# Background loads earlier and begun by ScalarE, high parts a step ahead of low parts

## The chip, the cores and the metric

The kernel runs on one core of a Trainium2 chip. The metric is the device time of one execution in microseconds (us). Five engines work beside each other, each through its own list of instructions in order: TensorE (PE in the profile; its weight loads are PEld), VectorE (DVE), ScalarE (ACT), GpSimd (POOL) and SyncE (SP), which only begins transfers. A transfer can be begun by SP or by ACT; each has a queue of its own, and the same 16 DMA engines move the bytes of both.

## The reference, cut to what matters

One transformer block for 2048 tokens of width 576, in float32. A vector `c` gives six modulation rows, attention has 32 heads of 128 that look at the last 512 cached keys (two heads share a cache), and a gated MLP of width 4608 follows.

```python
mod = (_silu(c) @ w_mod).reshape(c.shape[0], 6, 1, -1)
sa, ca, ga, sb, cb, gb = (mod[:, k] for k in range(6))
h = _layernorm(x) * (1 + ca) + sa
q = (h @ wq) per head
p = softmax(q @ k_cache[last 512] * Dh ** -0.5)
x = x + ga * ((p @ v_cache[last 512]) @ wo)
h = _layernorm(x) * (1 + cb) + sb
x = x + gb * ((sigmoid(h @ w_gate) * (h @ w_up)) @ w_down)
```

## The kernel before, in words

Each float32 product is made of three products of float32r parts: a value is split into a high part (ScalarE copies it rounded) and a low part (VectorE or GpSimd subtracts the high part from the value). The large products also use a seven-product scheme over 2 x 2 blocks (Strassen's), so weights are first added and subtracted with each other (the sums s1 to s4, t1 to t4) and then split.

The program is one loop over steps `n`, written out at build time. Steps -224 to -1 are the query projection (`q_step`, 7 products of 7 matmuls for each of 32 weight units). Steps 0 to 511 are attention, four steps for each block of 512 queries of one head: three matmuls of scores (`st`), four transposes of the probabilities (`pt`), three matmuls with the values (`ot`). After step 511 come the output projection and the MLP. Until then every engine keeps the order in which the program was written: `at_n(n, fn, ...)` puts a function at a step, ahead of that step's own products, and `at_late` behind them.

In one attention step ScalarE makes the exponentials (`pp<-st,neg`) and the rounded copy of the transposed probabilities (`ptt<-pt`), VectorE the maximum (`neg<-st`) and the low part of `ptt`, GpSimd the low part of the next queries (`qt`). Once in four steps the reciprocal sums `rs` go to a scratch in memory (`rscr<-rs`, `put_rs`) and come back spread over the partitions (`rb<-rscr`, `get_rs`); VectorE then multiplies the result `ot` by `rb` into `ov` (`ov_out`), and `put_o` stores `ov`.

Beside this runs background work, which prepares weights of later stages: 36 chunks `ab` of the gate and up weights, 9 chunks `tail` with their last rows, 16 `wo` and 18 `down` (these two are called wide here). A chunk has a room (a 128 x 2304 buffer: the `x` tiles and, in attention, four more called `xr`) or two. `bg_load` begins 4 transfers, `bg_sums` makes the sums on GpSimd in two parts, `bg_split` splits on ScalarE and GpSimd in two parts (not for `ab`), and `bg_store` begins 1 transfer (`ab`), 2 (wide) or 24 in four steps (`tail`, 6 in each step) to the scratches `wsc`, `wosc` and `dsc`. A planner sets the steps: a chunk is started at `n` when rooms are free and its due time is past, rooms are held for `HOLD` steps, and the due time moves on by a number for each kind. In the kernel before, all 636 of these transfers are begun by SP, between its other ones.

Weight units of the query projection are loaded raw by `load_raw` and `load_first` (SP), added by `w_sums` (GpSimd) and split by `w_split` (ScalarE, and right behind it VectorE). Finished queries go out by `q_store` (SP), from four buffers `qo`. `mod_fetch` loads one modulation row's weights (`wm`), `mod_sum` scales and adds them (ScalarE, GpSimd), and `mod_make2` ends with a matmul `st<-wm,ones`.

Of the kernel before, what the change touches and what calls it, by code (L numbers as in the profile page):

```python
# [16 lines left out]
P = 128  # L17
# [27 lines left out]
def adaln_block_kernel(ctx: ExitStack, tc: tile.TileContext, x, k_cache, v_cache, wq, wo, w_gate, w_up, w_down,  # L45
                       c, w_mod, out):
    early = [True]
    nc = Ordered(tc, early, tc.nc)
# [12 lines left out]
    D2 = D // 2  # L61
# [32 lines left out]
    def f32(ap):  # L94
        return ap.bitcast(F32)

    TQ = D2 - 2 * P
# [9 lines left out]
    def pin(i):  # L107
        if not early[0]:
            tc.keep_in_program_order(i)
# [4 lines left out]
    RAW = [qw.tile([P, 3, 4, P], F32, tag=f"raw{i}", name=f"raw{i}") for i in range(2)]  # L114
# [121 lines left out]
    A11, A12, A22, S1, S2, S4, S3, A21 = range(8)  # L236
# [55 lines left out]
    EARLY = 14  # L292
# [19 lines left out]
    WS, SWQ = {}, {}  # L312
# [11 lines left out]
            eng.tensor_sub(t[:, :, 0], raw_of(u, A12), WS[u, 0][:, :, 1])  # L324
            eng.tensor_sub(t[:, :, 1], raw_of(u, A11), raw_of(u, A21))

    def w_split(u, names, src, tail=None):
        tail = tail or nc.vector
        n = len(names)
        t = sw_tile([P, 5, 2, P]) if n == 2 else qw.tile([P, 5, 1, P], F32R, tag="sa", name="sa", bufs=2)  # L330
        nc.scalar.activation(t[:, 0:3], src, AF.Copy)
        nc.vector.tensor_sub(t[:, 3:5], src[:, 0:2], f32(t[:, 0:2]))
        r = slice(2 * TQ, 3 * TQ)
        tail.tensor_sub(t[r, 2], src[r, 2], f32(t[r, 2]))
        for i, a in enumerate(names):
            SWQ[u, a] = t[:, :, i, :]

    def w_split_first(u):
        w_split(u, (A11, A12), RAW[u // 2 % 2][:, :, u % 2 :: 2, :], nc.gpsimd if u else None)

    def w_split_a(u):
        w_split(u, (A11, A12), RAW[(u + 1) % 2][:, :, 0::2, :])

    def w_split_s(u, k):
        w_split(u, ((S1, S2), (S4, S3))[k], WS.pop((u, k)))

    def w_split_last(u):
        w_split(u, (A22,), RAW[(u + 1) % 2][:, :, 3:4, :])
# [151 lines left out]
    cols = {(h, s): ps_st() if 3 * h + s < 4 else ps_c() if s == 1 else ps_a() for h in range(2) for s in range(3)}  # L500
# [13 lines left out]
    for k in range(6):  # L514
        src = shift[0:1, k // 3 * D2 + k % 3 * P : k // 3 * D2 + (k % 3 + 1) * P] if k % 3 < 2 else \
# [13 lines left out]
    def at_n(n, fn, *args):  # L529
        at_step.setdefault(n, []).append((fn, args))  # L530
# [4 lines left out]
    def q_n(i):  # L535
        return NLO + i
# [15 lines left out]
    assert len(order) == NQ  # L552
    place = {x_: q_n(i) for i, x_ in enumerate(order)}
    for u in range(2, EARLY):
        at_n(max(place[u, A11] - 3, q_n(0)), w_split_first, u)
        if u >= 4:
            at_n(place[u // 2 * 2, A11] - 7, load_first, u)
    for u in range(2 * HKV):
        if u < EARLY:
            n = place[u, S1]  # L560
            at_n(n - 8, load_raw, u)
            times = (n - 4, n - 3), (n - 2, n), n + 1
        else:
            n = place[u, A11]
            at_n(n - (8 if u == EARLY else 10), load_raw, u)
            at_n(n - 3, w_split_a, u)
            times = (n - 4, n - 2), (n - 1, n + 1), n + 3
        for k in range(2):
            at_n(times[0][k], w_sums, u, k)
            at_n(times[1][k], w_split_s, u, k)  # L570
        at_n(times[2], w_split_last, u)


    CH = {}
# [441 lines left out]
    def bg_load(k, rooms):  # L1016
        kind, f = k
        if kind == "tail":
            raw = bg_view(rooms[0], 0, [4, P])
            BG[k] = raw, bg_view(rooms[0], 4 * P, [4, P]), bg_view(rooms[0], 8 * P, [7, P])  # L1020
            for slot, w, r0 in ((0, w_gate, 2 * P), (1, w_gate, D2 + 2 * P), (3, w_up, 2 * P), (2, w_up, D2 + 2 * P)):
                src = w[r0 : r0 + TQ, f * P : (f + 4) * P].rearrange("r (q n) -> q r n", q=4)
                pin(nc.sync.dma_start(raw[:, slot, :], src))
        elif kind == "ab":
            r = BG[k] = bg_view(rooms[0], 0, [8, 2, P])
            cols = slice(f * P, (f + 1) * P)
            for slot, w, r0 in ((0, w_gate, 0), (1, w_gate, D2), (2, w_up, D2), (7, w_up, 0)):
                pin(nc.sync.dma_start(r[:, slot], w[r0 : r0 + 2 * P, cols].rearrange("(s p) n -> p s n", p=P)))
        else:
            r = bg_view(rooms[0], 0, [8, D2])  # L1030
            BG[k] = r, bg_view(rooms[1], 0, [8, D2])
            w = wo if kind == "wo" else w_down
            for half, to in enumerate(((0, 1), (5, 2) if kind == "wo" else (7, 2))):
                for c, slot in enumerate(to):
                    r0 = (2 * f + c) * P
                    pin(nc.sync.dma_start(r[:, slot], w[r0 : r0 + P, half * D2 : (half + 1) * D2]))

    def bg_sums(k, part):
        kind, f = k
# [45 lines left out]
    def bg_store(k, part):  # L1085
        kind, f = k
        if kind == "tail":
            hi = BG[k][2]
            q = part
            rows = slice(q * TQ, (q + 1) * TQ)  # L1090
            for to in range(4):
                for a, b, src in bg_pairs(k) if to % 2 else [(0, 7, hi)]:
                    pin(nc.sync.dma_start(wsc[f + q][to * TQ : (to + 1) * TQ, a:b, 2, :], src[rows]))
        elif part == 0:
            if kind == "ab":
                pin(nc.sync.dma_start(wsc[f][:, :, 0:2], BG[k][:, 0:7]))
                return
            n = 8 if k == ("down", NF // 2 - 1) else 7
            for i in range(2):
                to = wosc[f // 4][:, :, f % 4, i].rearrange("c p d -> p c d") if kind == "wo" else dsc[f][:, i, :n]  # L1100
                pin(nc.sync.dma_start(to, BG[k][1 - i][:, :n]))


    XR = 4
# [5 lines left out]
    SPANS = {r: [(NLO + 27, NLO + 83), (ROOMS_FREE, N - 42)] if r < 2 else [(ROOMS_FREE, N - 42)] for r in range(NB)}  # L1110
    for r in range(NB, NB + XR):
        SPANS[r] = [(2, N - 42)]
    HOLD = {"ab": 14, "tail": 22, "wo": 22, "down": 22}
    free = {r: SPANS[r][0][0] for r in SPANS}
    n = NLO + 27
    due = float(n)
    while jobs or wide:
        assert n < N - 44, (n, len(jobs), len(wide))

        def fits(kind):  # L1120
            return [r for _, r in sorted((free[r], r) for r in SPANS if free[r] <= n and
                                         any(lo <= n and n + HOLD[kind] <= hi for lo, hi in SPANS[r]))]
# [24 lines left out]
    for b in range(NB):  # L1147
        at_n(max(free[b], N - 48 + 4 * b), load_x, b)
# [698 lines left out]
```

## Time and profile before

| what | value |
|---|---|
| median of 3 runs | 3193.76 us (3190.1 to 3196.66) |
| the profiled execution | 3193.45 us, its span 3191.5 us |
| granted TensorE clock, mean | 0.981 |
| PE busy | 3014.5 us (94%) |
| DVE, ACT, POOL busy | 2251.4 (71%), 1818.9 (57%), 1854.6 us (58%) |
| bytes moved | 637.28 MB, 200 GB/s over the span |
| first and last maximum of the scores | at 486.7 and 1571.8 us |

Nearly every instruction is recorded at line 36, a helper, so groups are told apart by their tiles. A name like `ptt<-pt` is output and input. The bracket behind a row of the timeline is the idle time ahead of it and what ended it. A DMA instruction's duration is the time that its queue (SPq, ACTq) spent on beginning it, not the transfer.

### The profile page before, as it was taken

Reading aid. Unit: us, or ns where it says so; the run is one execution under the profiler, and the core shown is the slowest. Engines: PE = TensorE matmul, PEld = TensorE weight load, DVE = VectorE, ACT = ScalarE, POOL = GpSimd, SP = SyncE. Lnnn points to the kernel's source line nnn. Section 1 sums busy time; section 2 is a strip of 40 time slices with the busy share of each in tenths; the row PEclk is TensorE's granted clock in tenths of the full one; section 3 lists DMA queues with packets and bytes.
Section 4 is the critical chain, followed back from the end, with each engine's and each line's share of the span. In section 5 each row is a group of like instructions: output and inputs, shape, how many; then the busy total and the mean of one; then the engine's idle time right before and its main releaser. Section 6 shows DMA issues by size and latency. Waiting matters only on the chain.

```text
span 3191.5 us, 50573 instructions
## 1 busy us (share of the span) xinstructions
PE 3014.5 (94%) x16375; PEld 2567.4 (80%) x16375; DVE 2251.4 (71%) x3908; ACT 1818.9 (57%) x3663; POOL 1854.6 (58%) x1685
## 2 busy tenths in 40 slices
PE   8878988789989998989999999999999999999999
PEld 6666766677777776777799998888888888888888
DVE  6767556667877776778788777666666686666667
ACT  5455446778878786767644555444444544444443
POOL 3745554578888885432255503676665566655555
PEclk9999999999999999999999999999999999999999
DMA  5855887878888888887654775655655565555554
GB/s 172 246 178 178 249 233 208 242 223 251 254 276 271 256 277 230 230 231 203 224 196 157 296 244 171 176 160 165 171 140 146 163 189 150 144 139 147 141 138 120
DMA packets 510087, 637.28 MB, mean 200 GB/s; under 512 B 56192, under 2 KB 429824, under 8 KB 501120
## 3 DMA queue, kind: packets, MB, share of 16 engines
q1 hardware_dynamic: 508688, 633.53, 66.5%
q8 instruction: 131, 2.15, 0.3%
q14 instruction: 132, 1.08, 0.1%
q10 hardware_dynamic: 1136, 0.53, 0.1%
HBM read 426.64 MB, written 207.25 MB: 199 GB/s over the span
## 4 chain that ended last, share of the span: by engine, by line
PE 63%; DMA 12%; DVE 7%; ACT 5%; issue 4%; POOL 4%; SPq 3%; ACTq 0%; POOLq 0%; DVEq 0%
PE a L36 22%; PE w L36 12%; PE c L36 11%; PE b L36 6%; PE ot L36 5%; PE st L36 4%; SPq L36 3%; DMA rb<-rscr 3%; PE pt L36 3%; DMA rscr<-rs 2%; DVE sw L36 2%; ACT pp L36 1%; ACT ptt L36 1%; DMA raw<-in_A_wq_dram 1%; POOL x L36 1%
## 5 line engine op out<-in xcount | busy, mean ns | idle before, releaser
L36 DVE TENSOR_TENSOR x<-w,x 128x288 f32<-128x288 f32 x964 | 418.8, 451 | 239.3 <-PE w L36 235.7
L36 PE MATMUL a<-hc,sw 128*128 128x512 f32 x2016 | 585.1, 396 | 1.4 <-DVE v L36 1.3
L36 PE MATMUL ot<-ptt,vs 128*128 128x512 f32 x1536 | 451.4, 403 | 56.2 <-DVE ptt L36 56.0
L36 PE MATMUL st<-kt,qt 128*128 128x512 f32 x1536 | 493.3, 430 | 3.0 <-POOL qt L36 3.0
L36 DVE TENSOR_TENSOR ptt<-pt,ptt 128x512 fp32r<-128x512 f32 x512 | 352.6, 689 | 191.6 <-ACT ptt L36 190.0
L36 ACT ACTIVATE pp<-st,neg 128x512 f32<-128x512 f32 x512 | 352.0, 687 | 175.2 <-DVE neg L36 172.3
L36 PEld LDWEIGHTS ot<-ptt,vs 128*128 128x128 f32 x1536 | 289.4, 192 | 143.6 <-DVE ptt L36 78.7
L36 PEld LDWEIGHTS a<-hc,sw 128*128 128x128 f32 x2016 | 356.4, 188 | 42.1 <-DVE v L36 3.2
L36 ACT ACTIVATE sw<-sr 128x384 fp32r<-128x384 f32 x504 | 257.4, 518 | 192.0 <-issue 90.5
L36 DVE TENSOR_REDUCE neg<-st 128x1 f32<-128x512 f32 x512 | 348.5, 681 | 6.2 <-PE st L36 6.2
L36 POOL TENSOR_TENSOR sw<-sr,sw 128x256 fp32r<-128x256 f32 x245 | 184.6, 754 | 281.0 <-ACT sw L36 276.0
L36 ACT ACTIVATE ptt<-pt 128x512 fp32r<-128x512 f32 x512 | 303.8, 593 | 77.0 <-PE pt L36 74.5
L36 PEld LDWEIGHTS pt<-ident,pp 128*128 128x128 f32 x2048 | 259.9, 143 | 100.1 <-ACT pp L36 29.8
L36 PEld LDWEIGHTS w<-wh,hl 128*128 128x128 f32 x1776 | 297.1, 188 | 52.7 <-DVE x L36 3.1
L36 PE MATMUL pt<-ident,pp 128*128 128x128 f32 x2048 | 313.5, 276 | 26.8 <-DVE rs L36 17.9
L36 PE MATMUL w<-wh,hl 128*128 128x288 f32 x1776 | 328.2, 296 | 0.8 <-DVE x L36 0.7
L36 POOL TENSOR_TENSOR qt<-qr,qt 128x512 fp32r<-128x512 f32 x128 | 165.8, 1295 | 273.4 <-ACT qt L36 191.3
L36 PE MATMUL c<-hc,sw 128*128 128x512 f32 x1008 | 304.0, 395 | 0.0
L36 DVE TENSOR_TENSOR sw<-sr,sw 128x256 fp32r<-128x256 f32 x259 | 187.9, 726 | 141.9 <-ACT sw L36 138.6
L36 PEld LDWEIGHTS st<-kt,qt 128*128 128x128 f32 x1536 | 256.4, 193 | 29.0 <-POOL qt L36 3.6
L36 POOL TENSOR_TENSOR hl<-vs,hl 128x512 fp32r<-128x512 f32 x139 | 191.8, 1380 | 108.1 <-ACT hl L36 106.1
L36 POOL TENSOR_TENSOR x<-x 128x256 f32<-128x256 f32 (+3 forms) x226 | 178.1, 805 | 74.4 <-DMA x<-in_B_w_up_dram 45.9
(295 smaller groups left out, 5895.9 us busy)
## 6 DMA issues: line engine op xcount, KB each, us to landing
sr<-wsc SPq DMA_DIRECT2D x504, 192.0 KB
wh<-dsc SPq DMA_DIRECT2D x144, 288.0 KB
qscr<-qo SPq DMA_DIRECT2D x128, 256.0 KB
qr<-qscr SPq DMA_DIRECT2D x128, 256.0 KB
vr<-oscr SPq DMA_DIRECT2D x32, 1024.0 KB
rb<-rscr SPq DMA_DIRECT2D x126, 256.0 KB
oscr<-ov SPq DMA_DIRECT2D x63, 512.0 KB
wsc<-x SPq DMA_DIRECT2D x26, 896.0 KB
```

The costliest lines, as they stand in the source:

```text
L36: i = got(*args, **kw)
```

## The change

Four things change.

1. `pin(nc.sync.dma_start(...))` in `bg_load` and `bg_store` becomes `pin(nc.scalar.dma_start(...))`: 636 transfers leave SP's list and enter ScalarE's: 144 loads and 36 stores of `ab` chunks, 36 and 216 of `tail`, 136 and 68 of the wide ones.
2. The planner: sums stand 11 or 12 steps behind the loads (6 before), stores 17 to 24 behind them (9 to 19), `HOLD` grows from 14/22 to 20/28/30, and the due times from 6.0/10.0/8.5 to 8.0/13.0 in the projection and 5.4/9.0/7.7 in attention. 16 chunks are started in the projection where it was 23.
3. In the projection `w_split` is cut in two: `w_hi` (ScalarE) stands a step ahead of `w_lo` (VectorE), raw loads and sums stand earlier, `q_store` a step later.
4. `mod_fetch` stands at steps 2, 26, 50, 74 (6, 30, 54, 78 before); what is made of it stands two steps later than before, so the load has 9 steps where it had 3.

```diff
-    def w_split(u, names, src, tail=None):
...
+    def w_hi(key, src, n=2):
         t = sw_tile([P, 5, 2, P]) if n == 2 else qw.tile([P, 5, 1, P], F32R, tag="sa", name="sa", bufs=2)
         nc.scalar.activation(t[:, 0:3], src, AF.Copy)
+        HALF[key] = t, src
+
+    def w_lo(key, u, names, tail=None):
+        t, src = HALF.pop(key)
         nc.vector.tensor_sub(t[:, 3:5], src[:, 0:2], f32(t[:, 0:2]))
...
-            at_n(n - (8 if u == EARLY else 10), load_raw, u)
-            at_n(n - 3, w_split_a, u)
-            times = (n - 4, n - 2), (n - 1, n + 1), n + 3
+            at_n(n - {EARLY: 10, EARLY + 1: 12}.get(u, 14), load_raw, u)
+            sums, his = (n - 5, n - 3), {2: n - 4, 4: n - 3, 0: n - 2, 1: n}
...
+        for k in his:
+            at_n(his[k], raw_hi if k in (2, 4) else sum_hi, u, k)
+            at_n(his[k] + 1, split_lo, u, k)
...
-                pin(nc.sync.dma_start(raw[:, slot, :], src))
+                pin(nc.scalar.dma_start(raw[:, slot, :], src))
...
-                    pin(nc.sync.dma_start(wsc[f + q][to * TQ : (to + 1) * TQ, a:b, 2, :], src[rows]))
+                    pin(nc.scalar.dma_start(wsc[f + q][to * TQ : (to + 1) * TQ, a:b, 2, :], src[rows]))
...
-    HOLD = {"ab": 14, "tail": 22, "wo": 22, "down": 22}
+    HOLD = {"ab": 20, "tail": 28, "wo": 30, "down": 30}
+    LEAD = {"ab": 11, "tail": 11, "wo": 12, "down": 12}
...
+        m = n + LEAD[kind]
         for part in range(2):
-            at_n(n + 6 + (part if kind == "ab" else 2 * part), bg_sums, k, part)
+            at_n(m + (part if kind == "ab" else 2 * part), bg_sums, k, part)
             if kind != "ab":
-                at_n(n + 10 + 3 * part, bg_split, k, part)
+                at_n(m + 5 + 3 * part, bg_split, k, part)
         for part in range(4 if kind == "tail" else 1):
-            at_n(n + (9 if kind == "ab" else 16 if kind == "tail" else 16) + part, bg_store, k, part)
-        due = max(due, n - 2) + {"ab": 6.0, "tail": 10.0}.get(kind, 8.5)
+            at_n(m + (6 if kind == "ab" else 12) + part, bg_store, k, part)
+        due = max(due, n - 2) + {"ab": 8.0 if n < 0 else 5.4, "tail": 13.0 if n < 0 else 9.0}.get(kind, 7.7)
...
-        n = 6 + 24 * k
+        n = 2 + 24 * k
         at_n(n, mod_fetch, m)
+        n += 6
...
-        while waiting and waiting[0] < n - 1:
+        while waiting and waiting[0] < n - 2:
```

Where a `tail` chunk is stored in attention, SP's list before has six stores to `wsc` at a step, then another chunk's loads, then `rb<-rscr` for the next `ov`, then six more stores:

```order
L36 DMA rscr_342<-rs 128x4
L36 DMA qr<-qscr_11_126 128x512
L36 DMA wsc_379<-xr_4292 224x1x128
L36 DMA wsc_379<-xr_4292 32x3x128
L36 DMA wsc_379<-xr_4292 32x4x128
L36 DMA wsc_379<-xr_4292 224x1x128
L36 DMA wsc_379<-xr_4292 32x3x128
L36 DMA wsc_379<-xr_4292 32x4x128
L36 DMA xr_4294<-in_B_w_gate_dram 128x2x128 x2
L36 DMA xr_4294<-in_B_w_up_dram 128x2x128 x2
L36 DMA rb<-rscr_342 128x512
```

Now such stores stand in ScalarE's list, here those of another `tail` chunk, six ahead of each step's rounded copy and exponential:

```order
L36 DMA wsc_376<-xr_4180 224x1x128
L36 DMA wsc_376<-xr_4180 32x3x128
L36 DMA wsc_376<-xr_4180 32x4x128
L36 DMA wsc_376<-xr_4180 224x1x128
L36 DMA wsc_376<-xr_4180 32x3x128
L36 DMA wsc_376<-xr_4180 32x4x128
L36 ACTIVATE ptt<-pt 128x4x128
L36 ACTIVATE pp,sum<-st,neg 128x512
```

SP's list is left with `rb`, `rs`, `qr`, `ov`, the caches and `wm` there. At a wide chunk ScalarE's list now has four loads of one chunk ahead of one step, the two stores of another ahead of the next, and then the first split of a third:

```order
L36 ACTIVATE qt<-qr 128x512
L36 DMA x_111<-in_A_wo_dram 128x288 x4
L36 ACTIVATE ptt<-pt 128x4x128
L36 ACTIVATE pp,sum<-st,neg 128x512
L36 DMA wosc_413<-xr_4178 128x7x288
L36 DMA wosc_413<-x_112 128x7x288
L36 ACTIVATE xr_4180<-xr_4179 128x1152
L36 ACTIVATE ptt<-pt 128x4x128
L36 ACTIVATE pp,sum<-st,neg 128x512
```

Before, ScalarE's list at such a place had the split alone, and the six transfers stood in SP's. In the projection VectorE's list changes like this in each weight unit (`sa` is the last block's split, `qo` a finished query block):

```order
-L36 TENSOR_TENSOR qo<-a,gate_976 128x512
-L36 TENSOR_TENSOR sw<-ws,sw 128x512
-L36 TENSOR_TENSOR sw<-ws,sw 32x256
 L36 TENSOR_TENSOR sa<-raw_76,sa 128x256
 L36 TENSOR_TENSOR sa<-raw_76,sa 32x128
+L36 TENSOR_TENSOR qo<-a,gate_985 128x512
+L36 TENSOR_TENSOR sw<-ws,sw 128x512
+L36 TENSOR_TENSOR sw<-ws,sw 32x256
```

The low part of the last block moved ahead of the query block and of one split; the high parts it subtracts stand a step earlier on ScalarE.

More of the change, by code (lines that the diff above doesn't have):

```diff
@@ L325, in w_sums, with first_hi, first_lo, raw_hi @@
             eng.tensor_sub(t[:, :, 1], raw_of(u, A11), raw_of(u, A21))
-    def w_split(u, names, src, tail=None):
-        tail = tail or nc.vector
-        n = len(names)
+    HALF = {}
+    def w_hi(key, src, n=2):
         t = sw_tile([P, 5, 2, P]) if n == 2 else qw.tile([P, 5, 1, P], F32R, tag="sa", name="sa", bufs=2)
         nc.scalar.activation(t[:, 0:3], src, AF.Copy)
+        HALF[key] = t, src
+    def w_lo(key, u, names, tail=None):
+        t, src = HALF.pop(key)
         nc.vector.tensor_sub(t[:, 3:5], src[:, 0:2], f32(t[:, 0:2]))
         r = slice(2 * TQ, 3 * TQ)
-        tail.tensor_sub(t[r, 2], src[r, 2], f32(t[r, 2]))
+        (tail or nc.vector).tensor_sub(t[r, 2], src[r, 2], f32(t[r, 2]))
         for i, a in enumerate(names):
             SWQ[u, a] = t[:, :, i, :]
+    def first_hi(u):
+        w_hi((u, 3), RAW[u // 2 % 2][:, :, u % 2 :: 2, :])
+    def first_lo(u):
+        w_lo((u, 3), u, (A11, A12), nc.gpsimd if u else None)
     def w_split_first(u):
[L339 to L348, printed above, removed]
+        first_hi(u)
+        first_lo(u)
+    def raw_hi(u, k):
+        w_hi((u, k), RAW[(u + 1) % 2][:, :, 0::2, :] if k == 2 else RAW[(u + 1) % 2][:, :, 3:4, :], 2 if k == 2 else 1)
+    def sum_hi(u, k):
+        w_hi((u, k), WS.pop((u, k)))
+    def split_lo(u, k):
+        w_lo((u, k), u, ((S1, S2), (S4, S3), (A11, A12), None, (A22,))[k])
     qscr = [[dram.tile([P, 4, BLK], F32, tag=f"qscr{h}_{g}", name=f"qscr{h}_{g}") for g in range(HKV)]
@@ L554, in adaln_block_kernel @@
     for u in range(2, EARLY):
-        at_n(max(place[u, A11] - 3, q_n(0)), w_split_first, u)
+        at_n(max(place[u, A11] - 4, q_n(0)), first_hi, u)
+        at_n(max(place[u, A11] - 3, q_n(0)), first_lo, u)
         if u >= 4:
@@ L560, in adaln_block_kernel @@
             n = place[u, S1]
-            at_n(n - 8, load_raw, u)
-            times = (n - 4, n - 3), (n - 2, n), n + 1
+            at_n(n - {0: 9, 1: 8}.get(u, 10), load_raw, u)
+            sums, his = (n - 4, n - 3), {0: n - 3, 4: n - 2, 1: n - 1}
         else:
             n = place[u, A11]
-            at_n(n - (8 if u == EARLY else 10), load_raw, u)
-            at_n(n - 3, w_split_a, u)
-            times = (n - 4, n - 2), (n - 1, n + 1), n + 3
+            at_n(n - {EARLY: 10, EARLY + 1: 12}.get(u, 14), load_raw, u)
+            sums, his = (n - 5, n - 3), {2: n - 4, 4: n - 3, 0: n - 2, 1: n}
         for k in range(2):
-            at_n(times[0][k], w_sums, u, k)
-            at_n(times[1][k], w_split_s, u, k)
-        at_n(times[2], w_split_last, u)
+            at_n(sums[k], w_sums, u, k)
+        for k in his:
+            at_n(his[k], raw_hi if k in (2, 4) else sum_hi, u, k)
+            at_n(his[k] + 1, split_lo, u, k)
     CH = {}
@@ L1027, in bg_load @@
             for slot, w, r0 in ((0, w_gate, 0), (1, w_gate, D2), (2, w_up, D2), (7, w_up, 0)):
-                pin(nc.sync.dma_start(r[:, slot], w[r0 : r0 + 2 * P, cols].rearrange("(s p) n -> p s n", p=P)))
+                pin(nc.scalar.dma_start(r[:, slot], w[r0 : r0 + 2 * P, cols].rearrange("(s p) n -> p s n", p=P)))
         else:
@@ L1035, in bg_load @@
                     r0 = (2 * f + c) * P
-                    pin(nc.sync.dma_start(r[:, slot], w[r0 : r0 + P, half * D2 : (half + 1) * D2]))
+                    pin(nc.scalar.dma_start(r[:, slot], w[r0 : r0 + P, half * D2 : (half + 1) * D2]))
     def bg_sums(k, part):
@@ L1092, in bg_store @@
                 for a, b, src in bg_pairs(k) if to % 2 else [(0, 7, hi)]:
-                    pin(nc.sync.dma_start(wsc[f + q][to * TQ : (to + 1) * TQ, a:b, 2, :], src[rows]))
+                    pin(nc.scalar.dma_start(wsc[f + q][to * TQ : (to + 1) * TQ, a:b, 2, :], src[rows]))
         elif part == 0:
             if kind == "ab":
-                pin(nc.sync.dma_start(wsc[f][:, :, 0:2], BG[k][:, 0:7]))
+                pin(nc.scalar.dma_start(wsc[f][:, :, 0:2], BG[k][:, 0:7]))
                 return
@@ L1100, in bg_store @@
                 to = wosc[f // 4][:, :, f % 4, i].rearrange("c p d -> p c d") if kind == "wo" else dsc[f][:, i, :n]
-                pin(nc.sync.dma_start(to, BG[k][1 - i][:, :n]))
+                pin(nc.scalar.dma_start(to, BG[k][1 - i][:, :n]))
     XR = 4
```

## The prediction

> **What bounds the kernel now.** I read the stages first (stretches of the profiled execution: length, busy time of each engine with its count, granted TensorE clock, DMA share, GB/s), then who waited for whom in each, then the timeline at the longest waits.
>
> ```profile
> core 0: us, PE busy (x) PEld busy (x) DVE busy (x) ACT busy (x) POOL busy (x), PEclk, DMA share, GB/s
> 30.00:490.00 460.00, 397.86 (x1637) 307.48 (x1637) 290.67 (x442) 222.55 (x366) 259.58 (x264) 0.95 0.69 206
> 490.00:700.00 210.00, 174.30 (x892) 139.71 (x891) 139.39 (x229) 148.79 (x342) 123.67 (x124) 0.93 0.80 228
> 700.00:1195.00 495.00, 464.41 (x2476) 374.96 (x2475) 383.56 (x617) 393.82 (x865) 417.60 (x322) 0.99 0.86 263
> 1195.00:1475.00 280.00, 249.96 (x1316) 203.59 (x1316) 205.21 (x330) 191.01 (x441) 122.33 (x127) 0.96 0.80 216
> 1580.00:3191.00 1611.00, 1603.58 (x9425) 1442.00 (x9423) 1129.76 (x2111) 774.51 (x1457) 900.78 (x817) 1.00 0.56 169
> ```
>
> From 1580 us on TensorE is busy throughout and the change touches nothing: term 0. Everything happens in the projection (to 490) and attention. There the pace tells what is lost:
>
> ```profile
> L36 DVE TENSOR_REDUCE neg<-st x512: 660/680/762, 486.7 to 1571.8; 128x1 f32<-128x512 f32 x171
> 912.39 0.95 PE L36 MATMUL st<-kt,qt 128*128 128x512 f32 x3
> 914.22 0.94 PE L36 MATMUL st<-kt,qt 128*128 128x512 f32 x3
> ```
>
> One maximum is one step: 1085.1 us over 511 steps are 2.12 us each, where two undisturbed steps stand 1.83 us apart. So attention loses 1085.1 - 511 x 1.83 = 150 us, in waits and in what follows them. The waits (engine, what it waited for: us, times, longest; the first three of the projection, the rest of attention):
>
> ```profile
> PE a L36 <- DVE qo L36: 19.4, 12, 4.1
> PE a L36 <- ACT gate L36: 16.6, 6, 8.4
> PE c L36 <- DVE ln_v L36: 9.2, 2, 7.5
> PE ot L36 <- DVE ptt L36: 56.0, 34, 8.1
> PE pt L36 <- DVE rs L36: 17.9, 3, 10.4
> PE st L36 <- POOL wm L36: 11.0, 4, 5.0
> DVE ov L36 <- DMA rb<-rscr: 35.2, 16, 8.3
> DVE ov L36 <- DMA oscr<-ov: 12.8, 5, 5.5
> ACT wm L36 <- DMA wm<-in_w_mod_dram: 20.4, 6, 9.7
> ```
>
> **What is removed.** First the wait of TensorE for `ot`. At the longest one:
>
> ```profile
> 1249.93 7.83 SPq L36 DMA_DIRECT2D wsc<-xr  x13
> 1257.86 1.59 SPq L36 DMA_DIRECT2D rb<-rscr  x1
> 1264.79 1.05 DVE L36 TENSOR_TENSOR ov<-ot,rb 128x512 f32<-128x512 f32 x1 [8.28 <-DMA rb<-rscr]
> 1267.09 1.65 PE L36 MATMUL ot<-ptt,vs 128*128 128x512 f32 x3 [8.12 <-DVE ptt L36]
> 1267.10:1270.30 3.20, 3.20 (x10) 2.61 (x11) 1.87 (x4) 2.08 (x7) 3.12 (x4) 0.50 0.98 308
> ```
>
> SP spends 7.83 us on beginning 13 stores of a `tail`, `rb` is begun behind them and lands 6.9 us later behind their bytes; VectorE stands 8.28 us at `ov`, everything behind it in its list (maxima, low parts) is late, and TensorE stands 8.12 us. The last row shows TensorE at clock 0.50 just after: 3.2 us at half speed cost another 1.6. With the stores out of SP's list, `rb` can be begun 7.83 us earlier, nearly the whole 8.28. VectorE's waits at `ov` sum to 35.2 + 12.8 = 48 us and TensorE's for `ot` to 56.0. I take 43 of the 56, since some of `rb`'s own round trip stays, and 7 for the half-clock stretches behind the four longest: **-50** (bounds: -15, if the full DMA engines alone make `rb` late, and -65).
>
> Second, `wm`. ScalarE stands 20.4 us before loads begun three steps (5.5 us at 1.83) ahead, its `pp` is late, and TensorE stands 17.9 and 11.0 us. Nine steps are 16.5 us; the longest wait was 9.7 over 5.5, that is 15.2. Of 28.9 I take 25, and 5 for half clock: **-30** (0 to -35). The fetch is put ahead of other transfers on SP by four steps; SP has fewer of them, so nothing is paid there.
>
> Third, the projection. Two of its long waits:
>
> ```profile
> 191.80 0.99 POOL L36 TENSOR_TENSOR ws<-raw 128x384 f32<-128x384 f32 x1 [12.05 <-DMA raw<-in_A_wq_dram]
> 419.39 3.54 SPq L36 DMA_DIRECT2D wsc<-x  x6
> 427.95 0.60 ACT L36 ACTIVATE qo<-b 128x512 f32<-128x512 f32 x1 [10.38 <-DMA qscr<-qo]
> 429.82 3.35 PE L36 MATMUL a<-qc,sw 128*128 128x512 f32 x7 [8.39 <-ACT gate L36]
> ```
>
> A raw load lands late and GpSimd's sums, the split and VectorE behind it wait (this is the 7.5 us of `ln_v`); or SP begins `tail` stores ahead of `qscr<-qo`, the buffers `qo` stay full, ScalarE stands 10.38 us, TensorE 8.39. Raw loads now stand 9 steps ahead of their sums (6 before), SP has no background transfers, and VectorE no longer meets a high part begun in the same step. Of the three rows' 45 us I take 22, and 8 for half clock and smaller waits: **-30** (0 to -45). The store a step later holds `qo` a step longer; four buffers at four per seven steps cover it; uncovered it is one wait of a step, 2 us, a unit.
>
> **What is paid.** 636 transfers are now begun by ScalarE. Rows for one (min/median/max ns):
>
> ```profile
> L36 ACTq DMA_DIRECT2D oscr<-ov x1: 597/597/597, 1581.5 to 1581.5; - x1
> L36 SPq DMA_DIRECT2D oscr<-ov x12: 518/520/617, 1407.2 to 1575.9; - x12
> L36 SPq DMA_DIRECT2D x<-in_A_wo_dram x32: 422/458/2184, 595.8 to 840.5; - x32
> L36 SPq DMA_DIRECT2D x<-in_B_w_down_dram x40: 449/1110/2949, 889.4 to 1185.5; - x40
> L36 SPq DMA_DIRECT2D dsc<-xr x16: 381/422/650, 954.1 to 1182.1; - x16
> ```
>
> and for ScalarE's and GpSimd's work in a wide stretch:
>
> ```profile
> 908.11 1.16 ACT L36 ACTIVATE x<-x 128x1152 fp32r<-128x1152 f32 x1
> 910.27 2.69 POOL L36 TENSOR_TENSOR x<-x,x 128x1152 fp32r<-128x1152 f32 x1
> 912.17 0.69 ACT L36 ACTIVATE pp<-st,neg 128x512 f32<-128x512 f32 x1 [0.72 <-DVE neg L36]
> 912.85 0.59 ACT L36 ACTIVATE ptt<-pt 128x512 fp32r<-128x512 f32 x1
> 914.04 0.92 ACT L36 ACTIVATE x<-x 128x864 fp32r<-128x864 f32 x1
> 915.03 2.06 POOL L36 TENSOR_TENSOR x<-x,x 128x864 fp32r<-128x864 f32 x1 [2.08 <-DMA rscr<-rs]
> 918.30 2.84 POOL L36 TENSOR_TENSOR x<-x,gate 128x576 f32<-128x576 f32 x2
> 921.21 3.22 POOL L36 TENSOR_TENSOR x<-x 128x288 f32<-128x288 f32 x4
> ```
>
> No row shows whether ScalarE computes while its list is at a transfer. `pp` starts right when `neg` ends (bracket: it stood for it), so there is no backlog, and I let only the `pp` in flight, about 0.9 us with its accumulator read, run beside.
>
> A `tail` in attention: 24 stores at 7.83 / 13 = 0.60 us are 14.5 us in four steps that take 4 x 1.83 = 7.3; ScalarE's 1.3 us per step mostly fit under them. It falls 7.2 us behind. `pp` is made two steps ahead of its transposes; of those 3.7 us I count 2.7 as spare, so TensorE loses 4.5. Ten `tail` chunks' worth (9, with some half clock): **+45** (0 if hidden; +75 with no spare and half clock each).
>
> A wide chunk: four loads at 0.47 are 1.9 us, 0.9 of it beside `pp`; two stores at 0.42 fit beside the next `pp`. One us is left. Over 7.7 steps (14.1 us) ScalarE has 7.7 x (1.28 + 0.16 for `qt`) + 1.16 + 0.92 = 13.2 us, so this fills it; I count 0.45 for each of 34: **+15** (0 to +88: at 1.11 us a load, as behind full queues, 2.6 more on each). The stores also wait for GpSimd's last subtraction, four steps before; what stands behind them is `ptt`, for which VectorE and then `ot` wait. GpSimd has 2.84 + 3.22 + 2.69 + 2.06 + 2.5 for `qt` = 13.3 us in those 14.1: full, and no bound yet; term 0, at worst 34 us if each chunk falls a us behind. The `ab` chunks, four loads and one store in 5.4 steps with no split: **+5** (0 to +20).
>
> [...]
>
> Sum: -50 - 30 - 30 + 45 + 15 + 5 = **-45**; 3193.45 - 45 = 3148 us. The profiled execution stands 0.3 us from the median (3193.76), so this is the forecast of the median too.
>
> **The rivals.** *Hidden issue*: ScalarE goes on with two steps' `pp` and `ptt` already handed to it (3.5 us of time) while transfers are begun. A `tail`'s 7.2 us are then covered but for 1 (2.7 spare, 3.5 backlog), a wide chunk's wholly: cost 10 in place of 65, so -100, 3093 us. [...] For it: ScalarE is busy only 393.82 of 495 us in the fullest stage. Against: it often waits for `neg`. *ScalarE becomes the bound*: with loads stretched to 1.11 us, because two queues fill the same engines (share 0.86 already), the wide chunks cost 88 in place of 15; +28, 3221 us. It decides once a wide chunk costs 1.8 us: 34 of them are then 60, which with 45 and 5 is the whole gain of 110. For it: 14.1 us are just full. Against: loads now mostly stand ahead of the stores, not behind. [...] *`rb` stays late*, since the engines are full and not SP: -15 in place of -50, 3183 us.
>
> **How the numbers follow.** Forecast 0.50 (alone 3115 to 3185), hidden issue 0.27, ScalarE the bound 0.14, `rb` stays late 0.09. 0.2% (6 us) is about what a measurement of this kernel can tell. Faster: 0.27 + 0.46 + 0.04 = 0.77; same 0.04 + 0.04 = 0.08; slower 0.15 (the bound's 0.14, and 0.01). The range 3085 to 3205 takes in the first two cases and the last, and leaves out most of the bound's.
>
> **What would show it.** Right: no `ACT wm` wait for its load and none of TensorE's for `wm`; VectorE's wait at `ov` under 10 us; GpSimd's for `raw` nearly gone; TensorE's longest waits in attention at the `tail` stores, with ACTq solid there. Wrong: ScalarE computing at its usual pace through the ACTq rows (hidden issue), or wide steps at 2.1 us and more with ACTq rows of over a us (the bound), or `ov` waiting for `rb` as before.

## The result, and the profile after

The changed kernel takes 3362.32 us in the median (3360.58 to 3366.07), 1.0522 of the time before (95% interval 1.0509 to 1.0534): 169 us slower, where 3148 was forecast. The profiled execution spans 3360.0 us.

The first and the last maximum of the scores, and the stages cut there (stretch, its length, busy time (count) of each engine, granted TensorE clock, DMA share, GB/s):

```profile
L36 DVE TENSOR_REDUCE neg<-st x512: 658/680/703, 476.2 to 1740.4; 128x1 f32<-128x512 f32 x171
```

```profile
core 0: us, PE busy (x) PEld busy (x) DVE busy (x) ACT busy (x) POOL busy (x), PEclk, DMA share, GB/s
30.00:476.00 446.00, 393.40 (x1629) 305.50 (x1627) 271.83 (x439) 218.92 (x360) 225.48 (x231) 0.95 0.62 191
476.00:1740.00 1264.00, 1041.25 (x5182) 823.43 (x5182) 808.84 (x1302) 807.66 (x1816) 704.82 (x618) 0.92 0.73 214
1760.00:3360.00 1600.00, 1592.34 (x9341) 1430.82 (x9340) 1122.48 (x2100) 770.27 (x1450) 899.90 (x816) 1.00 0.56 168
```

The same stretches of the kernel before:

```profile
30.00:487.00 457.00, 394.86 (x1630) 305.16 (x1629) 290.29 (x442) 221.77 (x364) 259.58 (x264) 0.95 0.69 207
487.00:1572.00 1085.00, 983.02 (x5182) 795.41 (x5183) 809.35 (x1302) 806.24 (x1813) 684.97 (x587) 0.97 0.82 241
```

The projection ends 10.5 us earlier (486.7 to 476.2). Attention takes 1264.2 us in place of 1085.1: all of the loss, and more. Behind it nothing changed. ScalarE computes as much in attention as before (808 and 806 us), so it has no more work to do there. TensorE, with the same 5182 matmuls, is idle for 1264.0 - 1041.25 = 223 us where it was 102, which is 121 of the 179 us. The other 58 are matmuls that take longer, 1041.25 for 983.02, at a granted clock of 0.92 for 0.97.

Who waits in attention now (the first, third and fourth have their counterparts in the prediction; ACT is ScalarE):

```profile
PE ot L36 <- DVE ptt L36: 97.0, 54, 7.9
PE pt L36 <- DVE ptt L36: 71.8, 45, 5.3
PE pt L36 <- DVE rs L36: 29.3, 14, 7.6
PE st L36 <- POOL wm L36: 16.6, 4, 7.4
...
DVE ptt L36 <- ACT ptt L36: 415.7, 342, 10.1
...
ACT ptt L36 <- DMA wsc<-xr: 53.2, 14, 8.1
ACT ptt L36 <- DMA wsc<-x: 26.6, 8, 6.8
ACT ptt L36 <- DMA qr<-qscr: 15.9, 6, 4.1
ACT ptt L36 <- DMA sscr<-sx: 10.0, 1, 10.0
```

The second row and the one of VectorE were, in the kernel before:

```profile
PE pt L36 <- DVE ptt L36: 1.7, 5, 0.5
DVE ptt L36 <- ACT ptt L36: 189.5, 324, 12.2
```

VectorE's waits at `ov` for `rb` and `oscr` (48 us) have no row any more, and ScalarE's for `wm`'s load none either: what was to be removed is gone. In their place VectorE stands 415.7 us for ScalarE's copy `ptt`, where it stood 189.5, and ScalarE stands ahead of that copy behind transfers. All its rows of that kind sum to 172 us in 42 waits; before there was none. The copy uses nothing of `wsc`, `qr` or `sscr`: what stood at these transfers is the list ahead of it. From the timeline of attention I added up ScalarE's idle stretches that end with a transfer of its list: 99 of them, 274 us. In 158 us of these a transfer was being begun; in the other 116 the list stood ahead of a transfer or between two. By kind it is 74 us at the loads and 52 at the stores of wide chunks, 74 at the loads of `ab` and `tail`, 75 at their stores.

One `tail` in the timeline (ACTq: ScalarE's queue, beginning transfers):

```profile
1399.38 4.66 ACTq L36 DMA_DIRECT2D wsc<-xr  x5
...
1404.09 0.60 ACT L36 ACTIVATE ptt<-pt 128x512 fp32r<-128x512 f32 x1 [4.74 <-DMA wsc<-xr]
...
1404.72 0.69 DVE L36 TENSOR_TENSOR ptt<-pt,ptt 128x512 fp32r<-128x512 f32 x1 [5.05 <-ACT ptt L36]
...
1405.56 1.08 PE L36 MATMUL pt<-ident,pp 128*128 128x128 f32 x4 [3.64 <-DVE ptt L36]
...
1406.29 1.63 PE L36 MATMUL st<-kt,qt 128*128 128x512 f32 x3
```

and TensorE's clock around it:

```profile
1399.00:1405.50 6.50, 2.79 (x13) 2.00 (x13) 1.45 (x4) 1.61 (x5) 0.00 (x0) 0.94 0.95 284
1405.50:1412.00 6.50, 6.40 (x20) 4.91 (x20) 1.95 (x4) 1.78 (x4) 2.28 (x3) 0.54 0.53 133
```

Five stores are begun in 4.66 us (the first of the six ran beside `pp`); for 4.74 us ScalarE does nothing, VectorE and TensorE behind it do nothing, and when TensorE goes on its clock is 0.54 for the next 6.5 us: three matmuls take 1.63 us for 0.95. Work handed over ahead, as the rival *hidden issue* has it, shortens nothing behind the stores here: `ptt`, next in the list, starts at 1404.09, when the row of stores has ended (1404.04).

In the projection the stores to `wsc` now hold ScalarE, and through `gate` TensorE. TensorE's waits for `gate` in the first block of products (`a`) are as long as before (15.8 us in the first row, 16.6 before), while GpSimd's for `raw` fell from 50.9 to 11.1:

```profile
PE a L36 <- ACT gate L36: 15.8, 6, 7.5
PE c L36 <- ACT gate L36: 8.3, 3, 4.1
ACT gate L36 <- DMA wsc<-x: 13.0, 3, 6.3
POOL ws L36 <- DMA raw<-in_A_wq_dram: 11.1, 2, 6.1
```

### The profile page after: what moved, and what is told of

It is laid out like the page before. It is cut to its first block, busy times and chain, and to the rows that moved or that the text cites. A ratio compares the mean times of both kernels' runs of the same rounds, so it can differ in the third digit from the quotient of the medians.

```text
span 3360.0 us, 50493 instructions
## 1 busy us (share of the span) xinstructions
PE 3071.0 (91%) x16375; PEld 2595.8 (77%) x16375; DVE 2234.3 (66%) x3908; ACT 1818.6 (54%) x3663; POOL 1841.9 (55%) x1685
## 4 chain that ended last, share of the span: by engine, by line
PE 54%; POOL 7%; DMA 7%; issue 4%; ACT 4%; DVE 3%; ACTq 2%; SPq 0%; POOLq 0%; DVEq 0%
PE a L36 19%; PE w L36 12%; PE c L36 10%; PE b L36 5%; PE ot L36 3%; PE st L36 3%; POOL x L36 3%; PE pt L36 2%; ACTq L36 2%; DMA qr<-qscr 2%; ACT pp L36 1%; POOL xr L36 1%; ACT ptt L36 1%; POOL qt L36 1%; DMA oscr<-ov 1%
## 5 line engine op out<-in xcount | busy, mean ns | idle before, releaser
L36 PE MATMUL ot<-ptt,vs 128*128 128x512 f32 x1536 | 470.5, 417 | 97.3 <-DVE ptt L36 97.0
L36 PE MATMUL st<-kt,qt 128*128 128x512 f32 x1536 | 511.9, 443 | 3.4 <-POOL qt L36 3.4
L36 PEld LDWEIGHTS ot<-ptt,vs 128*128 128x128 f32 x1536 | 300.2, 200 | 194.9 <-DVE ptt L36 127.4
L36 PE MATMUL pt<-ident,pp 128*128 128x128 f32 x2048 | 328.3, 285 | 105.7 <-DVE ptt L36 75.0
L36 PEld LDWEIGHTS st<-kt,qt 128*128 128x128 f32 x1536 | 267.4, 201 | 31.3 <-POOL qt L36 4.3
L36 POOL TENSOR_TENSOR x<-x 128x288 f32<-128x288 f32 (+3 forms) x236 | 182.3, 790 | 28.6 <-ACT x L36 17.6
```

The source lines that it names most:

```text
L36: i = got(*args, **kw)
```

## The experiments

Ratios are to the kernel before on the same chip, each with its 95% interval. A difference of two ratios is turned into us with 3190.

**Which part carries it.** Four kernels move only the queue of background transfers.

*All on SP*: the changed kernel with

```diff
-                pin(nc.scalar.dma_start(...   # bg_load, bg_store
+                pin(nc.sync.dma_start(...
```

> The changed kernel with all loads and stores of background chunks begun by SP again; the planner, the high parts a step ahead and the earlier fetch stay. Theory A (ScalarE's list stands while a transfer is begun): the 275 us that ScalarE idles behind its transfers in attention go, and the gains of the other parts show: 3140 to 3175 us. Rival B (the planner: denser chunks fill GpSimd and the DMA engines): stays above 3300 us.

3202.87 us, 1.0039 (1.0027 to 1.0051): between the two expectations. Nearly the whole loss goes with the queue, but the other parts leave no gain.

*Queue alone*: the kernel before with the opposite edit in `bg_load` and `bg_store`.

> The kernel before with one edit: background loads and stores begun by ScalarE. Theory A: the whole loss comes with it, 3340 to 3400 us (loads then also stand behind stores and six steps ahead of their sums, so it may be more than the change). Rival B: at most 3230 us.

3390.69 us, 1.0633 (1.0612 to 1.0655). As theory A had it: neither the planner nor the split of the weights is needed for the loss.

*Tail stores on SP*: the changed kernel with the 216 `tail` stores alone given back to SP.

> The changed kernel with only the 216 stores of tail chunks begun by SP. Theory A, by issue time: ScalarE idles 76 us behind stores to wsc in attention and 38 in the projection; most of it comes back, 3362 - 90 = about 3270 us, with rb late at the tails again (some 20 us of that lost): 3270 to 3290. Rival C (it is waits of single transfers for GpSimd and for earlier transfers, not the count of them): 3330 to 3362 us.

3304.37 us, 1.0363 (1.0342 to 1.0383), between the two expectations.

*Stores on SP*: all 320 stores given back, the loads left on ScalarE.

> The changed kernel with all 320 stores begun by SP, and the 316 loads by ScalarE. Theory A by issue alone: 64 + 10 us of attention and 28 of the projection come back, 3362 - 100 = about 3260 us. Rival C (waits count): the whole idle time behind stores, 76 + 52 + 38, comes back: about 3200 us.

3280.8 us, 1.0289 (1.0268 to 1.0309), again between the two. By these, the step from 1.0522 to 1.0039 (154 us) falls to 51 us for the tail stores, 24 for the other stores, and 80 for the loads. Each is net: with stores on SP the waits for `rb` return, in the kernel with all on SP to more than before:

```profile
DVE ov L36 <- DMA rb<-rscr: 46.0, 25, 6.8
DVE ov L36 <- DMA oscr<-ov: 36.0, 8, 11.5
PE ot L36 <- DVE ptt L36: 74.8, 42, 10.8
```

**The other parts.** *Projection and fetch*: the projection's part and the earlier fetch on the kernel before, old planner, all on SP.

> The changed kernel with two of its four parts undone: background transfers begun by SP again, and the planner's old steps; left are the projection part (high parts a step ahead, raw loads earlier, queries stored a step later) and the earlier fetch of the modulation weights. Theory A (the loss is the queue's, and these two parts are a gain of their own): the first maximum stands some 15 to 20 us earlier, as with everything on SP (466.7 against 486.7), and attention loses ScalarE's wait for wm (20 us), so 3150 to 3170 us. Theory B (the projection's gain came from the planner's fewer chunks in the projection, 16 in place of 23): first maximum at 480 to 487, and 3180 to 3195.

3168.63 us, 0.9936 (0.9917 to 0.9955). The time is as theory A had it; the first maximum, at 477.0, lies between the two expectations: 9.7 us in the projection.

*Planner alone*: the kernel before with the new `HOLD`, `LEAD` and due times, all on SP.

> The kernel before with the new planner's steps alone, all transfers still begun by SP. Theory A (the planner gives room in the projection and takes it back in attention): attention at about 1120 us as with everything on SP, the first maximum at about 480, so 3210 to 3230 us. Theory B (the planner's fewer chunks are what frees the projection, the split of the weights gives nothing): first maximum at 467 to 470, 3200 to 3208. Theory C (the planner is harmless, and the earlier fetch or the earlier raw loads collide with rb in attention): 3185 to 3195.

3205.28 us, 1.0058 (1.0043 to 1.0073). First maximum at 464.4, last at 1581.7. The planner gives 22.3 us in the projection, more than the weights' part, and takes 32 back in attention (1117.3 us for 1085.1), where seven chunks more now stand. Both expectations had half of it.

*Fetch alone*: `mod_fetch` four steps earlier, its sums two later.

```diff
-        n = 6 + 24 * k
+        n = 2 + 24 * k
         at_n(n, mod_fetch, m)
+        n += 6
```

> The kernel before with the modulation weights fetched four steps earlier and used two steps later, nothing else. By the prediction's step: ScalarE's wait for wm (20.4 us) gone and 30 us less, 3163. Theory A (about a third of it: attention was 11.5 us shorter with this and the projection part together): 3180 to 3188, the ACT wm wait gone but TensorE's for wm behind GpSimd still there (11 to 14 us). Theory B (nothing): 3190 to 3196.

3181.35 us, 0.9973 (0.9961 to 0.9985), some 9 us, as theory A had it. ScalarE's wait for the load is gone, and so is TensorE's of 17.9 us behind `rs`. TensorE's for `wm` isn't (11.0 before): GpSimd, which makes the other half of the sum, now stands for ScalarE's half:

```profile
PE st L36 <- POOL wm L36: 14.3, 4, 6.3
POOL wm L36 <- ACT wm L36: 12.3, 4, 11.0
```

In the same profile, of an execution of 3188.76 us, TensorE's waits for `ot` are 63.8 us, where they were 56.0.

**The price of a transfer by itself.** The kernel before gets 234 more transfers of 128 x 4 values (0.5 MB in all), begun by ScalarE in steps 96 to 329.

```diff
+    TINY = [const.tile([P, 4], F32, name=f"tiny{i}") for i in range(4)]
+    def tiny(i):
+        pin(nc.scalar.dma_start(TINY[i % 4], w_mod[i % 4 * P : (i % 4 + 1) * P, 0:4]))
+    for i in range(234):
+        at_n(96 + i, tiny, i)            # bursts: 96 + i // 4 * 4
```

*One to a step*:

> The kernel before, and ScalarE begins 234 more transfers of 128 x 4 values from the modulation weights, one ahead of each step from 96 to 329 (their values go nowhere). Their bytes are next to nothing (0.5 MB), so this is the price of beginning a transfer on ScalarE, spread evenly, beside the wide chunks. Theory A (ScalarE's list stands while a transfer is begun): 234 x 0.5 us = 117 us of ScalarE's list; a step has 1.83 us and ScalarE 1.3 to 1.7 of work in it, so a half to a fifth of it shows: +25 to +60 us, 3215 to 3255. Theory B (what is already handed over runs beside it): +0 to +8. Theory C (the changed kernel lost by its stores and loads waiting in the list, not by beginning them): +0 to +8.

3243.59 us, 1.0176 (1.0161 to 1.0191), +56 us.

*The same in bursts of four*:

> As the kernel with 234 small transfers begun by ScalarE, but four of them in a row ahead of every fourth step, the same number over the same steps, as the changed kernel's wide loads stand. Theory A (the list stands through a burst of 2 us, and TensorE has some 2.7 us of spare): 58 bursts; the list catches up where the step has spare time, so at most that of the spread ones and up to twice: +25 to +110 us, and more than spread where the first 0.9 us of each beginning run beside pp. Theory B (handed-over work runs beside): a burst of four hides less well than single ones, +5 to +30. Theory C (waits, not beginning): +0 to +8.

3301.18 us, 1.0352 (1.0335 to 1.0368), +112 us, 1.9 us a burst. One burst:

```profile
939.30 0.85 ACTq L36 DMA_DIRECT2D tiny<-in_w_mod_dram  x2
...
940.25 1.56 ACTq L36 DMA_DIRECT2D tiny<-in_w_mod_dram  x2
...
941.85 0.60 ACT L36 ACTIVATE ptt<-pt 128x512 fp32r<-128x512 f32 x1 [1.88 <-PE st L36]
...
942.48 0.69 DVE L36 TENSOR_TENSOR ptt<-pt,ptt 128x512 fp32r<-128x512 f32 x1 [2.18 <-ACT ptt L36]
...
943.32 0.63 PE L36 MATMUL pt<-ident,pp 128*128 128x128 f32 x4 [0.78 <-DVE ptt L36]
```

Four transfers are some 2.5 us of the list, 1.5 of it the beginnings themselves and 0.8 a wait ahead of the last one. Some 0.6 lies beside the `pp` that was running (ScalarE is idle 1.88), and over the 58 bursts about as much as the rest comes out as time. The prediction had the six transfers of a wide chunk cost 0.45 us.

*Own tiles* (twelve tiles in turn, so that no small transfer waits for its tile), one to a step and in bursts:

> As the kernel with 234 small transfers spread one to a step (3243.6 us), but with twelve tiles in turn in place of four, so that none waits in ScalarE's list for the landing of an earlier one. Theory A (the beginning itself costs, 0.24 us of the 0.37 it takes): 3230 to 3245. Theory C (a transfer that waits in the list for its tile was what cost): 3190 to 3205.

> As the kernel with small transfers in bursts of four (3301.2 us), but with twelve tiles in turn, so that none waits for the landing of an earlier one. Theory A (ScalarE's list stands through the burst and TensorE has no spare of 2.7 us): 3285 to 3305, 1.7 to 1.95 us a burst. Theory C (waits for the tiles): 3190 to 3230.

3240.0 us, 1.0162 (1.0148 to 1.0175), and 3301.02 us, 1.0354 (1.0341 to 1.0367): the wait for the tile was no part of it. Durations of one (min/median/max ns), in the bursts a third more:

```profile
L36 ACTq DMA_DIRECT2D tiny<-in_w_mod_dram x234: 334/335/928, 715.5 to 1240.8; - x117
```

```profile
L36 ACTq DMA_DIRECT2D tiny<-in_w_mod_dram x234: 334/443/1697, 716.8 to 1304.5; - x117
```

The single ones cost by something else than their beginning: of 84 us of it, 67 lie beside ScalarE's work by the timeline, and yet they cost 52. What they add is waiting ahead of the beginning, some 65 us in 48 idle stretches of ScalarE. The worst one (SP's four loads are shown in two rows, as they were begun; DVE and PE rows left out but for the last):

```profile
1005.16 1.28 SPq L36 DMA_DIRECT2D x<-in_B_w_down_dram  x3
1010.00 0.33 SPq L36 DMA_DIRECT2D x<-in_B_w_down_dram  x1
...
1010.42 0.35 ACTq L36 DMA_DIRECT2D tiny<-in_w_mod_dram  x1
...
1010.83 0.60 ACT L36 ACTIVATE ptt<-pt 128x512 fp32r<-128x512 f32 x1 [5.69 <-DMA rscr<-rs]
...
1012.29 1.09 PE L36 MATMUL pt<-ident,pp 128*128 128x128 f32 x4 [5.64 <-DVE ptt L36]
```

ScalarE had ended its work at 1005.14; a transfer that takes 0.35 us was begun 5.3 us later. The program's lists give the reason: every transfer uses one of eight completion counters, in turn over both queues (the trace of the changed kernel has 2495 transfers on eight, 312 or 311 on each), and each of the small ones waits for its counter's last use. In this kernel's list of ScalarE, with what each waits for (`DMAHW0` to `DMAHW7` are the counters):

```
L36 DMA tiny0_417<-in_w_mod_dram 128x4 [waits DMAHW7_49]
L36 ACTIVATE ptt_6966<-pt_6967 128x4x128 [waits PE_49]
L36 ACTIVATE pp_6974,sum_6918<-st_6958,neg_6917 128x512 [waits DVE_49,Activation_49]
L36 DMA tiny1_418<-in_w_mod_dram 128x4 [waits DMAHW1_49]
```

By that each small transfer in ScalarE's list waits for the landing of another, eight before it, of whatever engine. The trace bears it out: the transfer above was begun 0.02 us after the landing of `rscr<-rs` was counted on its counter, the bracket behind `ptt` names the same landing, and SP's own fourth load stood from 1006.44 to 1010.00 too. Of the 43 waits over 0.3 us in these stretches, 64 us in all, 40 with 60 us end that way, 0.02 us behind a landing. SP's own beginnings do not account for these waits: of the 5.3 us ahead of the 0.35 us record SP was beginning something in 1.5. Over all 64 us SP was beginning something in 22, and it does so in 41% of the stage anyway.

The changed kernel has such waits as well: in attention its list stood 92.5 us ahead of transfers in waits of over 0.3 us, and 65.6 of them end 0.02 us behind a landing on the transfer's counter; the other 26.9 all stand at stores. With the queue alone moved it is 93 of 97 us. No run changed the number of the counters, so what these waits are worth in time wasn't measured by itself.

*Another place in the list*, behind `ptt` and ahead of `pp`, singles and bursts (twelve tiles):

```diff
             transp(n)
+        for i in MID.pop(n, ()):
+            tiny(i)
         if 0 <= n + 2 < N:
             expo(n + 2)
```

> The 234 small transfers spread one to a step (twelve tiles in turn; 3240.0 us when ahead of ptt), now begun behind ptt and ahead of pp in ScalarE's list. Theory P (what decides is ptt's small spare, 0.9 us ahead of ot and 1.4 us ahead of its bank's reuse, and pp has 2.5): 3190 to 3215. Theory T (ScalarE's time as a whole is short, the place doesn't matter): 3232 to 3246.

> The bursts of four (twelve tiles in turn; 3301.0 us when ahead of ptt), now begun behind ptt and ahead of pp. Theory P: pp is late by 1.6 us out of 2.5, the next ptt by 1.6 less the half us that ScalarE idles in a step, so 0.2 to 0.8 us a burst: 3200 to 3240. Theory T: 3290 to 3305.

3227.63 us, 1.0126 (1.0109 to 1.0143), and 3284.91 us, 1.0303 (1.0288 to 1.0319). Both lie outside the expectations, near those of theory T: the place is worth 11 of 52 and 16 of 113 us. The small spare of `ptt` is a part of the price and not its reason; `pp` has as little to give.

*The same transfers begun by SP*, singles and bursts:

> The 234 small transfers, one to a step (3240.0 us when begun by ScalarE), begun by SP at the same steps. Theory T (the price is that ScalarE's list stands for them): within 10 us of before, 3185 to 3200. Theory S (they delay the other transfers, by the eight shared counters or the queues): 3220 to 3245.

> The bursts of four (3301.0 us when begun by ScalarE), begun by SP at the same steps. Theory T: within 15 us of before, 3185 to 3205. Theory S: 3260 to 3305.

3223.08 us, 1.0106 (1.0091 to 1.0121), and 3229.16 us, 1.0135 (1.0117 to 1.0152). Neither expectation holds whole. Begun by SP they cost 34 and 43 us, in bursts little more than spread. Whether SP's fuller list does it or the counters, which come round sooner, isn't separated. The kernel with the single ones on SP, between 714 and 1260 us:

```profile
PE ot L36 <- DVE ptt L36: 46.5, 32, 6.1
DVE ov L36 <- DMA rb<-rscr: 25.5, 18, 2.2
PE st L36 <- DMA kv<-in_A_k_cache_dram: 11.4, 4, 4.2
```

and the kernel before between the same us:

```profile
PE ot L36 <- DVE ptt L36: 29.3, 23, 5.7
DVE ov L36 <- DMA rb<-rscr: 10.9, 10, 2.7
PE st L36 <- DMA kv<-in_A_k_cache_dram: 4.9, 4, 2.4
```

So what it costs more to begin them by ScalarE is only 18 us for the single ones (1.0162 against 1.0106), and 70 for the bursts (1.0354 against 1.0135).

**Versions.** *Tail stores spread, on SP*: the kernel with the projection's part and the fetch, the 24 stores of a `tail` two in each of twelve steps.

```diff
-    HOLD = {"ab": 14, "tail": 22, "wo": 22, "down": 22}
+    HOLD = {"ab": 14, "tail": 28, "wo": 22, "down": 22}
...
-        for part in range(4 if kind == "tail" else 1):
+        for part in range(12 if kind == "tail" else 1):
```

> The projection part and the earlier fetch on the kernel before, all background transfers on SP, and the 24 stores of a tail two in each of twelve steps (six in each of four before); a tail's room is held 28 steps, the chunks start as before. Theory A (the stores in a row in SP's list are what delays rb): VectorE's waits at ov for rb and oscr fall from 51 us (38.9 and 12.0 with the projection part and the fetch alone) to under 20, TensorE's for ot from 61.0 by as much, and 3168.6 becomes 3125 to 3145 us. Theory B (the full DMA engines delay rb, whoever begins it): the waits stay over 40, 3160 to 3175.

3144.89 us, 0.986 (0.9845 to 0.9874), the best of all. Its waits in attention, and those without the spreading:

```profile
PE ot L36 <- DVE ptt L36: 41.0, 32, 6.4
DVE ov L36 <- DMA rb<-rscr: 19.0, 14, 3.9
```

```profile
PE ot L36 <- DVE ptt L36: 61.0, 35, 8.1
DVE ov L36 <- DMA rb<-rscr: 38.9, 16, 8.1
```

The waits for `rb` and `oscr` fall from 51 to 39 us, less than expected (`oscr` rose from 12.0 to 19.9), TensorE's for `ot` by 20, the time by 24 us (0.9936 to 0.986). Some 6 of these lie in the projection, where `tail` stores were spread too (first maximum at 470.8 for 477.0).

*Pairs on SP, pairs on ScalarE*: the same, and loads two in each of two steps, the stores of a wide chunk one in each of two; the second kernel begins all of them by ScalarE and differs in nothing else.

> As the kernel with the spread tail stores (3144.9 us), and the four loads of every background chunk two in each of two steps, the two stores of a wide chunk one in each of two; all begun by SP. Theory A (rows of transfers in SP's list delay rb and ov's store; 39 us of VectorE's waits at ov are left): 3125 to 3140. Theory B (what is left of the waits is the full DMA engines'): 3140 to 3150.

> The same program with at most two background transfers a step, all begun by ScalarE as in the changed kernel. Some 480 of the 636 stand in attention. Theory T (a transfer costs ScalarE's list 0.2 us when single and more in pairs, wherever it stands): 480 x 0.2 to 0.35 = 100 to 170 us over the same program on SP, 3230 to 3310. Theory R (only long rows of them cost, and pairs run beside pp): within 25 us of it, 3130 to 3165.

3144.38 us, 0.9867 (0.985 to 0.9883), and 3283.49 us, 1.0298 (1.0283 to 1.0314). The second, in attention:

```profile
PE ot L36 <- DVE ptt L36: 55.8, 58, 4.2
PE pt L36 <- DVE ptt L36: 68.3, 48, 5.9
```

and the first:

```profile
PE ot L36 <- DVE ptt L36: 40.8, 34, 4.4
PE pt L36 <- DVE ptt L36: 6.4, 7, 3.2
```

On SP the time is as theory B had it: spreading further gives nothing more. Even so thinly spread, the same transfers cost 137 us more when they are ScalarE's, as theory T had it: the queue is the cause, not the length of its rows alone. In that kernel ScalarE stands 79 us ahead of transfers in attention in waits over 0.3 us, and 76 of them end behind a landing on the transfer's counter.

## Why the prediction was wrong

- **The step that failed** is what a begun transfer costs on ScalarE: +65 in the sum. The net price of the move is 154 us, and gross it is higher, since `rb`'s gain is in it. The durations of one were right (0.56 us median for a `tail` store, 0.33 to 0.53 for loads and wide stores); what they displace was not, and the waits ahead of them had no term. I set ScalarE's sum of work (13.2 us) against the length of a wide chunk's steps (14.1), and counted 2.7 us of `pp`'s spare. ScalarE's time isn't short: it is busy 808 of 1264 us. But the scores, maximum, exponential, transposes and copies of the following steps wait for one another, two of these stand in its list, and a stop of 2 us there reached TensorE nearly whole (1.9 us a burst of four, where 0.45 was counted for a wide chunk). The loads, priced at next to nothing, cost 80 us.
- **Half clock** was counted with the waits removed (7, 5 and part of 8 us); of those made, a part of 4.5 us at the `tail` chunks and the rest only inside the bounds. It is 58 of attention's 179 us. In the kernel with bursts on twelve tiles it is a third too: the matmuls between 716 and 1307 us take 482.95 us for 446.41 before (714 to 1191), at a clock of 0.95 for 0.99.
- **Waits in the list**: the prediction has a remark on stores that wait for GpSimd, and no term. Of the 274 us that ScalarE idles at its transfers in attention 116 are waits and not beginnings, and most of the longer ones are for the landing of an unrelated transfer on the same counter (65.6 of 92.5 us), which nothing in the prediction has.
- **The planner** had no term either: by itself it costs 0.58%, some 18 us, 22 less in the projection and 32 more in attention. With all transfers on SP `wm` and the projection should have left 60 us of gain; that kernel is 12 us slower than before.
- **`rb` (-50)**: right as a mechanism. With the stores out of SP's list VectorE's 48 us of waits are gone, and the rival that the DMA engines make `rb` late did not come (DMA share 0.73, no wait). It isn't refuted for fuller engines: the share was 0.82 before, and on SP, where it stays at 0.83 with the stores spread, 39 us of these waits stay too. There 12 of 51 us of them less came with 24 us less time. The whole term was not measured by itself.
- **`wm` (-30)**: the wait went as said, the time didn't: 9 us. I took 25 of 28.9 us from ScalarE's lateness. The 17.9 behind `rs` went, but TensorE's 11.0 for `wm` stayed with GpSimd's half of the sum, and its waits for `ot` grew by 7.8.
- **Projection (-30)**: 10.5 us with the transfers on ScalarE, 20.0 with them on SP (first maximum at 466.7). Part and planner overlap: 9.7 and 22.3 alone.
- **Rivals**: hidden issue is refuted as a forecast. Its mechanism is there in part (67 of 84 us of the single transfers' beginning lie beside ScalarE's work), but no run shows its 3.5 us handed over ahead: at the `tail` above one store of six ran beside `pp`, and ScalarE stood for 4.74 us ahead of `ptt`. The waits ahead of a transfer are not hidden either (some 65 us of ScalarE's idle time at the single ones). ScalarE as the bound had the direction, and its condition, 1.8 us for a wide chunk, is met: 125 us of idle behind 34 of them is 3.7. But it gave 3221, because it counted only what the chunks exceed ScalarE's free time by.
- **The marks** named for a wrong forecast came: rows of ACTq of well over a us (3.4 at most for a load of `wo`). Of those for a right one, VectorE's short waits at `ov`, ScalarE's at `wm` and GpSimd's for `raw` came, and TensorE's for `wm` at none did not. TensorE's longest wait (7.9 us) stands at a `tail`'s stores, but waits of 6 to 7.6 stand at loads and stores of wide chunks too.

## What to carry to other kernels

A transfer belongs into the list of an engine that nothing waits for: here, in the list of one that stands in every step's chain, the wait ahead of it, and what of its beginning did not run beside that engine's work, came out as time for the most part (179 us of attention, for 274 us that ScalarE idled at transfers), although that engine was busy only 808 of 1264 us. Look up what the transfer itself waits for: here, for 60 of the 64 us of a small one's longer waits, it was the landing of another on its counter, eight before it. When a row of transfers in a queue makes an urgent one late, spread the row over more steps in the same queue before moving it to another (here 24 us won, against 154 lost). When pricing a wait, follow the chain through that engine to the bound one, and add the clock that it loses after each stop (here 0.54 over the 6.5 us behind a stop of 3.64 us).

## What the runs showed of the hardware that was not expected

- The stop of TensorE of 3.64 us that ends at 1405.5 is followed by a clock of about half: 0.54 over the next 6.5 us. Over attention the mean clock fell from 0.97 to 0.92.
- Small transfers begun one by one took 0.335 us each in ScalarE's queue (median), in bursts of four 0.443, and up to 1.7. Of the burst above the first pair took 0.85 us and the second 1.56, 0.8 of it a wait.
- A small transfer in ScalarE's list stood for 5.3 us for the landing of `rscr<-rs`, with which it shares nothing but the completion counter, and everything behind it in the list stood with it.
